# A fused attention and two-expert kernel: another order in the first pairs, decoding spread over the pair, a free bank for the second h, and half of w1 through DRAM

## The chip, the cores and the metric

The kernel runs on one core of a Trainium2 chip. Its engines are TensorE (PE in the profile: matrix products and transposes into PSUM banks), VectorE (DVE), ScalarE (ACT), GpSimd (POOL) and SyncE (SP, which only issues DMAs here). The metric is the device time of one execution, in microseconds (us); the time of a kernel is the median of three runs.

## The reference, cut to what matters

Attention with a memory term, and behind it two experts in a row. All arrays come as 64-bit floats.

```python
# q, k, v (4, 8, 576, 64), M_prev (4, 8, 64, 64), z_prev (4, 8, 64), beta (8)
scores = where(causal, -1e9, scale * q @ k.T)      # causal is the part above the diagonal
a = exp(scores - scores.max(-1)); a /= a.sum(-1) + 1e-9
phi = lambda x: where(x > 0, x, exp(x) - 1) + 1
mem = (phi(q) @ M_prev) / ((phi(q) * z_prev).sum(-1) + 1e-6)
g = 1 / (1 + exp(-beta))
x = heads_to_columns(g * mem + (1 - g) * (a @ v))  # 2304 tokens x 512

h = x @ w_in                                       # w_in 512 x 2048
x = (h * tanh(softplus(h))) @ w_out                # w_out 2048 x 512

out = ((x @ w1) * (x @ w2)) @ w3 @ w_out2          # w1, w2 512 x 1024; w3 1024 x 1024; w_out2 1024 x 512
```

## The kernel before

**Attention.** The 32 heads are worked in 16 pairs `p`, one round of the loop at L568 each; a round computes the scores of pair p and, between them, the transposes and the value products of pair p - 1. The rows of scores come in blocks of 128 queries: `s_blocks` (L402) makes blocks 3, then 2, then 0 and 1 together, `s_last` (L418) the 64 queries that are left of both heads (s4). PE writes the products into a bank pair of psA; DVE takes them with one custom instruction that adds the mask and finds the minimum (`maxed`, L395), ACT makes the exponential and its sum (`expd`, L400), and `normed` (L373) scales each block by the reciprocal of its sum, on DVE or, for four of them, on POOL (L384). `pt_g` (L443) transposes the scaled blocks on PE into psF, and ACT copies them (L452). `pv` (L454) multiplies by v and splits the result into x's high and low half (L473 and L474).

The memory term: `phi_terms` (L332) makes phi(q) with ACT (L340), POOL (L341), DVE (L342) and the product with z on POOL (qz, L345), which is held back behind the last scaling on POOL (`scaled`); `phi_norm` (L350) sums (L354), takes the reciprocal (L356), applies the gate (L357) and multiplies on POOL (phie, L360); `trans_phi` (L365) transposes it. `prep` (L316) transposes q and k of the next pair into psX, ACT copies them (L318), and POOL masks the last queries (qd, L324).

**Weights.** A 64-bit word is made into a 32-bit float by six DVE operations (L110, 111, 114, 117, 120, 121) and one POOL addition (L125); the result is then rounded to a high half (L76) and the rest taken as a low half (L79 or L170), both on POOL, since every product of the experts is made of three products of such halves. One job is a block of 128 rows by 512 columns. The eight jobs of the first quarter of w_in and w_out are done in pairs 4 to 11, one in each, by `drip` (L551): it takes a job's operations from the list `parts` and places some of them behind the DVE instruction in `taken`, the last take of scores. The words lie in two buffers `draw`, the decoded block in one buffer `da` (`decoder(at, 2, 1)`).

**The experts.** The first expert runs in four quarters `g` of 512 hidden columns by six chunks `n` of 384 tokens: `h_steps` (L478) makes h in four parts m, each of twelve products into half of a psA bank pair, and applies the function on ACT and DVE (L498 to 511); `split_y` splits it; `emit_x2` (L660) multiplies by w_out and DVE adds into x2 (L675, L677). Beside it `run(pre, ...)` decodes weights of the second expert into DRAM (`predecode`, L189: w_out2 and the first halves of w1 and w2), and `fold` (L682) multiplies w3 by w_out2 in the last quarter and sends the product through DRAM into `wft`. In the second expert `emit_ab` (L807) makes a and b from x2's halves and the slots w12t of w1 and w2, `emit_out` (L826) the output, five steps later. The second halves of w1 and w2 are decoded straight into the slot by `second_half` (L194), two jobs at each call of `by_two` (L150), between the end of the first expert and the first steps of the second.

**The order.** Each engine works through its instructions in one fixed order. A scheduler sets it from the program, and `tc.issue_after(x)` tells it that what is recorded in the block comes behind x. `in_turn` (L68) does so on PE with its last product, if `ordered[0]` is set, which it is from pair 1 on. PSUM has the tags A (two pairs of banks), X (two banks) and F (two banks).

Of the kernel before, what the change touches and what calls it, by code (L numbers as in the profile page):

```python
# [21 lines left out]
def fused_kernel(ctx: ExitStack, tc, q, k, v, M_prev, z_prev, beta, w_in, w_out, w1, w2, w3, w_out2, out):  # L22
# [8 lines left out]
    NQ = 4  # L31
# [118 lines left out]
    def by_two(jobs):  # L150
        for _ in range(4):
            run(jobs, 2)
            yield
# [33 lines left out]
    w2_dram = dram.tile([2, DM, WN], F32, name="w2_dram")  # L187

    def predecode():  # L189
# [34 lines left out]
    decoder(at, 2, 1)  # L224
# [107 lines left out]
    def phi_terms(p):  # L332
# [58 lines left out]
    scaled = [None]  # L391
    copied = [None]
# [61 lines left out]
    def pv(p):  # L454
# [16 lines left out]
        for o, q0, q1 in ((pm, 0, 512), (pl, 512, S)):  # L471
            x = xl[b // 2][:, :, c, S * (b % 2) + q0:S * (b % 2) + q1]
            nc.scalar.copy(out=x[:, 0], in_=o[:, 0:q1 - q0])  # L473
            sub(x[:, 1], o[:, 0:q1 - q0], x[:, 0])  # L474
# [3 lines left out]
    def h_steps(u):  # L478
# [72 lines left out]
    def drip(n):  # L551

        if not parts and ahead:
            r, done = ahead.pop(0)
            ops, a, flat = decode_ops(r)

            def last():
                ops[6]()
                done(a, flat)

            parts.extend(ops[0:6] + [last])
        with tc.issue_after(taken[0]):
            for op in parts[:n]:
                op()
        del parts[:n]

    pre = predecode()
    for p in range(NPAIR + 1):  # L568

        now, old, new = p < NPAIR, p > 0, p + 1 < NPAIR  # L570
        ordered[0] = 1 <= p
# [9 lines left out]
        decodes = 4 <= p < 12  # L581
# [9 lines left out]
        if old:  # L591
            in_turn(pt_g, p - 1, 1)
            in_turn(pt_g, p - 1, 0)
            if not now:
                in_turn(next, h0)
        if now:
            in_turn(s_blocks, p, (2,))
            if old:
                with tc.issue_after(taken[0]):
                    normed(p - 1, [(4, None)])  # L600
                    phi_norm(p)
        if p == 0:
            gate_values(b_)
# [5 lines left out]
        if new:  # L609
            in_turn(prep, p + 1, "q")  # L610
        if old:
            in_turn(pt_g, p - 1, 3)
        if now:
            in_turn(s_blocks, p, (0, 1))
            if decodes:
                drip(1)
        if new:
            in_turn(prep, p + 1, "k")
        if old:
            in_turn(pt_g, p - 1, 5)  # L620
            in_turn(pt_g, p - 1, 6)
            if not now:
                in_turn(next, h0)
        if p == 1:
            in_turn(trans_phi, 0)
# [5 lines left out]
        if p == 0:  # L631
# [11 lines left out]
        if decodes:  # L643
            drip(7)
# [15 lines left out]
    def emit_x2(u, beside):  # L660
# [4 lines left out]
        for m in range(KD):  # L665
            o = bank("X" if g == NQ - 1 else "XF"[m % 2])[:, 0:CH]
# [65 lines left out]
    def w_slot(s):  # L732
        t = xp.tile([128, 2, 2, KD, 512], F32R, tag=f"xs{s}", name="w12t", padded_shape=[128, 2, 2, KD, S])
        if s == 0:
            for i, wd in enumerate((w1_dram, w2_dram)):
                from_dram(t[:, i], wd)
        w1t[s], w2t[s] = t[:, 0], t[:, 1]
        return t

# [4 lines left out]
    for u in [(g, n) for g in range(NQ) for n in range(NCH)]:  # L744
        g, n = u
        last = g == NQ - 1
        if u not in gt:
# [5 lines left out]
        if last and n == 3:  # L753
            w_slot(0)
        if prev is not None:
            with tc.issue_after(emit_x2(prev, folding if last and n > 0 else pre0)):
                split = split_y(u, y)
        with tc.issue_after(split):
# [4 lines left out]
            if g in (1, 2) and n in (0, 2):  # L763
# [15 lines left out]
    rest = by_two(second_half(w_slot(1)))  # L779
    emit_x2(prev, islice(rest, 1))  # L780
# [64 lines left out]
    for k, (c, m) in enumerate(work):  # L845
# [10 lines left out]
        if k < 3:  # L856
            steps(rest, 1)
# [38 lines left out]
```

## Time and profile before

| | us |
|---|---|
| median of three runs | 1013.98 (1013.22 to 1014.81) |
| the profiled execution, its own time | 1015.02 |
| its span in the trace | 1013.2 |

The busy time of each engine in the span, from the page:

| engine | busy us | share | instructions |
|---|---|---|---|
| PE | 973.4 | 96% | 5584 |
| DVE | 605.5 | 60% | 1380 |
| ACT | 500.8 | 49% | 1016 |
| POOL | 331.8 | 33% | 329 |

The shares are means over stages that differ: attention until about 250 us, the first expert until about 740 us, the second behind it. DVE is busy 60 to 90 per cent in most of the attention and the first expert and 10 to 30 per cent in the second. What sets the time of a stage is read from the waits in it.

### The profile page before, as it was taken

What the parts mean: (1) busy time and instruction counts of PE and PEld (TensorE: products, weight loads), DVE (VectorE), ACT (ScalarE), POOL (GpSimd) and SP (SyncE); (2) the same over time, 40 slices, a digit from 0 to 9 for tenths busy, and PEclk for the clock granted to TensorE, in tenths of its full rate; (3) what the DMA queues carried; (4) which work ended last, traced back from release to release, by engine and by line L of the source; (5) the groups of instructions that cost most, each with busy time, mean ns of one, the idle gap of its engine ahead of it and who ended that gap; (6) DMA issues with size and microseconds to landing.
All of it is one profiled execution on the core that took longest, in us unless ns stands there. A gap on an engine that the chain in (4) does not pass through costs nothing.

```text
span 1013.2 us, 15098 instructions
## 1 busy us (share of the span) xinstructions
PE 973.4 (96%) x5584; PEld 826.9 (82%) x5584; DVE 605.5 (60%) x1380; ACT 500.8 (49%) x1016; POOL 331.8 (33%) x329
## 2 busy tenths in 40 slices
PE   6899889999999999999999999999879999999998
PEld 4565555567999999999999999988658888888897
DVE  4678888873657578967896666666973121121111
ACT  5788788886655555555656544432322221221112
POOL 4456677752252536453545111112540000000000
PEclk8999999999999999999999999999999999999999
DMA  7534443301221233223321672222500100100101
GB/s 155 121 72 95 117 119 86 81 15 63 83 81 45 84 125 123 85 98 111 125 84 63 228 260 73 83 79 79 177 21 0 42 1 1 43 1 5 38 1 63
DMA packets 93626, 81.73 MB, mean 81 GB/s; under 512 B 68720, under 2 KB 72816, under 8 KB 93552
## 3 DMA queue, kind: packets, MB, share of 16 engines
q1 hardware_dynamic: 92224, 80.44, 26.2%
q8 instruction: 44, 0.72, 0.3%
q10 hardware_dynamic: 1328, 0.33, 0.2%
q14 instruction: 30, 0.25, 0.1%
HBM read 65.54 MB, written 15.20 MB: 80 GB/s over the span
## 4 chain that ended last, share of the span: by engine, by line
PE 71%; DVE 12%; POOL 7%; ACT 6%; issue 2%; DMA 2%; POOLq 0%; SPq 0%; DVEq 0%; ACTq 0%
PE psA L63 37%; PE psX L63 17%; PE psF L63 14%; ACT s L400 2%; POOL s L384 2%; DVE s L395 2%; POOL da L125 2%; PE psF L66 1%; DMA draw<-in_moe_w_dram 1%; DVE da L117 1%; DVE da L110 1%; POOL qz L345 1%; ACT pt L452 1%; DVE da L111 1%; DVE da L114 1%
## 5 line engine op out<-in xcount | busy, mean ns | idle before, releaser
L63 PE MATMUL psA<-xt,wqt 128*128 128x384 f32 x1152 | 207.4, 335 | 2.3 <-DVE y L511 2.2
L125 POOL TENSOR_TENSOR da<-da,draw 128x512 f32<-128x512 f32 x72 | 100.8, 1407 | 325.2 <-DVE draw L121 283.0
L63 PEld LDWEIGHTS psA<-xt,wqt 128*128 128x128 f32 x1152 | 200.1, 188 | 3.8 <-DVE y L511 3.1
L63 PE MATMUL psX<-gh,wqt 128*128 128x384 f32 x480 | 122.2, 335 | 1.1 <-DVE x L677 1.1
L822 DVE TENSOR_TENSOR bs<-bs,psA 128x512 f32<-128x512 f32 (+1 forms) x40 | 25.3, 633 | 161.7 <-ACT bs L821 161.7
L63 PE MATMUL psA<-x2h,w12t 128*128 128x512 f32 (+1 forms) x384 | 108.3, 360 | 6.9 <-DVE bs L822 4.6
L821 ACT COPY bs<-psA 128x512 f32<-128x512 f32 (+1 forms) x40 | 21.8, 545 | 163.3 <-PE psA L63 153.4
L400 ACT ACTIVATE s<-s,acc 128x512 f32<-128x512 f32 (+2 forms) x144 | 85.2, 597 | 19.2 <-DVE acc L395 18.3
L63 PE MATMUL psA<-x2s,w12t 128*128 128x512 f32 x384 | 89.6, 389 | 0.0
L63 PEld LDWEIGHTS psX<-gh,wqt 128*128 128x128 f32 x480 | 86.8, 188 | 2.3 <-DVE x L677 1.4
L63 PEld LDWEIGHTS psA<-x2h,w12t 128*128 128x128 f32 x384 | 69.0, 191 | 21.1 <-DVE bs L822 5.0
L498 ACT ACTIVATE y<-psA 128x384 f32<-128x384 f32 x96 | 42.0, 490 | 88.8 <-PE psA L63 88.7
L63 PEld LDWEIGHTS psA<-x2s,w12t 128*128 128x128 f32 x384 | 72.1, 188 | 15.0
L511 DVE TENSOR_TENSOR y<-y,psA 128x384 f32<-128x384 f32 x96 | 48.5, 548 | 54.2 <-ACT y L509 54.2
L63 PE MATMUL psX<-gl,wqt 128*128 128x384 f32 x240 | 80.3, 335 | 0.0
L395 DVE CUSTOM_DVE_ANT_0 s<-psA,mask 128x512 f32<-128x512 f32 (+2 forms) x144 | 63.4, 482 | 25.8 <-PE psA L63 25.5
L66 PEld LDWEIGHTS psF<-ident,s 128*128 128x128 f32 x400 | 44.1, 143 | 41.3 <-ACT pt L452 11.9
L66 PE MATMUL psF<-ident,s 128*128 128x128 f32 x400 | 62.9, 289 | 10.8 <-DVE s L384 6.2
L63 PE MATMUL psF<-gh,wqt 128*128 128x384 f32 x288 | 73.0, 334 | 0.0
L384 POOL TENSOR_SCALAR s<-s,sum,ogp 128x128 f32<-128x128 f32 (+1 forms) x64 | 53.6, 849 | 46.3 <-DVE sum L380 30.5
L63 PE MATMUL psA<-room,w12t 128*128 128x512 f32 (+1 forms) x192 | 68.6, 357 | 0.0
L452 ACT COPY pt<-psF 128x512 f32<-128x512 f32 (+1 forms) x112 | 58.5, 543 | 13.3 <-PE psF L66 13.3
(117 smaller groups left out, 1866.7 us busy)
## 6 DMA issues: line engine op xcount, KB each, us to landing
draw<-in_moe_w_dram SPq DMA_DIRECT2D x32, 512.0 KB, 3.8
draw<-in_moe_w_out_dram SPq DMA_DIRECT2D x24, 512.0 KB, 3.6
draw<-in_moe_w_in_dram SPq DMA_DIRECT2D x16, 512.0 KB, 4.6
out_dram<-ob SPq DMA_DIRECT2D x18, 256.0 KB, 2.0
raw<-in_q_dram SPq DMA_DIRECT2D x32, 128.0 KB, 2.8
raw<-in_v_dram SPq DMA_DIRECT2D x32, 128.0 KB, 2.7
o_dram<-draw SPq DMA_DIRECT2D x8, 512.0 KB, 2.8
w_dram<-draw SPq DMA_DIRECT2D x8, 512.0 KB, 2.9
```

The source lines that it names most:

```text
L63: tail[0] = nc.tensor.matmul(o, lhsT=l, rhs=r, start=start, stop=stop).ins
L66: tail[0] = nc.tensor.transpose(o, src, ident).ins
L110: lambda: V.tensor_scalar(out=ai, in0=hw, scalar1=0x7FFFFFFF, scalar2=None, op0=ALU.bitwise_and),
L125: lambda: nc.gpsimd.tensor_tensor(out=a, in0=a, in1=lw.bitcast(F32), op=ALU.add),
L384: r = (nc.gpsimd if x in ON_POOL else nc.vector).tensor_scalar(out=s, in0=s, scalar1=d["sum"][:, x:x + 1], scalar2=og[:, x:x + 1], op0=ALU ...
L395: taken[0] = nc.vector.tensor_tensor_reduce(out=s, in0=o, in1=m, op0=ALU.add, op1=ALU.min, scale=-scale, scalar=init, accum_out=a,).ins
L400: nc.scalar.activation(out=s, in_=s, func=AF.Exp, scale=-1.0, bias=a, accum_out=r)
L452: copied[0] = nc.scalar.copy(out=t[:, 0:n], in_=o[:, 0:n]).ins
L498: nc.scalar.activation(out=y[m // 2][:, m % 2], in_=hp[m], func=AF.Tanh, scale=0.5)
L511: nc.vector.tensor_tensor(out=y[i][:, j], in0=y[i][:, j], in1=hp[2 * i + j], op=ALU.mult)
L821: nc.scalar.copy(out=bs, in_=pb)
L822: nc.vector.tensor_tensor(out=bs, in0=bs, in1=pa, op=ALU.mult)
```

## The change

- **First pairs.** In pair 0, phi of pair 0 and the transposes of q and k for pair 1 are placed between the scores; qz of pair 0 is not held back behind a scaling; PE's order is fixed from pair 0 on; `trans_phi(0)` moves to the front of pair 1. The block scalings of a pair are placed behind the last take of scores.
- **Decoding in the pairs.** `drip` places the first three operations behind the scores of blocks 0 and 1, the fourth behind the split of x in `pv`, the fifth behind block 3 of the next pair, and the sixth with POOL's three behind block 2 of the next pair. There are two buffers `da`.
- **Second h.** The first part m of h for (g, n) = (0, 1) goes into a psX bank; the other three follow in psA. `emit_x2` of (0, 0) uses the banks X, F, F, X. In the last round of the pair loop one step of the first h moves ahead of `pt_g` 5 and 6.
- **w1's second half.** Its four jobs become part of `predecode`, into a new array `w1b_dram` (written job by job, read back by two DMAs). The number of jobs of `predecode` grows from 16 to 20 and `run(pre, 1)` is called at more chunks. What `second_half` still decodes is w2's four jobs; its slot is taken at the last chunk of the last quarter, and its steps alternate there with those of `fold` (`both`).

The core of the diff; what is left out are the moved calls of the pair loop, which the orders below show.

```diff
     def by_two(jobs):
-        for _ in range(4):
+        for _ in range(2):
...
+        for c in range(KD):
+            yield words(w1, 128 * c, WN), to_dram(w1b_dram[:, 128 * c:128 * c + 128, 0:WN])
...
     def second_half(t):
-        for i, w in ((1, w2), (0, w1)):
-            for c in range(KD):
-                yield words(w, 128 * c, WN), to_split(t[:, i, 0, c], t[:, i, 1, c])
+        for c in range(KD):
+            yield words(w2, 128 * c, WN), to_split(t[:, 1, 0, c], t[:, 1, 1, c])
...
-    decoder(at, 2, 1)
+    decoder(at, 2, 2)
...
-        with tc.issue_after(scaled[0]):
+        with ExitStack() as k_:
+            if p > 0:
+                k_.enter_context(tc.issue_after(scaled[0]))
...
         for m in range(KQ):
-            if m % 2 == 0:
-                two = psA()
-            o = two[:, m % 2, 0:CH]
+            j = m - (u == (0, 1))
+            if j < 0:
+                o = psX()[:, 0:CH]
+            else:
+                if j % 2 == 0:
+                    two = psA()
+                o = two[:, j % 2, 0:CH]
...
         if now:
             in_turn(s_blocks, p, (3,))
-            if decodes:
-                drip(1)
+            drip(1, taken[0])
+            if p == 1:
+                in_turn(trans_phi, 0)
...
+        else:
+            gate_values(b_)
+            phi_terms(0)
+            in_turn(prep, 1, "q")
         if now:
             in_turn(s_blocks, p, (2,))
-            if old:
-                with tc.issue_after(taken[0]):
+            drip(2, taken[0])
+            with tc.issue_after(taken[0]):
+                if old:
                     normed(p - 1, [(4, None)])
-                    phi_norm(p)
+                phi_norm(p)
...
         if now:
             in_turn(s_blocks, p, (0, 1))
-            if decodes:
-                drip(1)
-        if new:
+            if 4 <= p < 12:
+                begin()
+                drip(3, taken[0])
+        if old and new:
             in_turn(prep, p + 1, "k")
...
             in_turn(s_last, p)
-            if decodes:
-                drip(1)
-            normed(p, [(i, e) for e in range(2) for i in range(4)])
-        if p == 0:
             with tc.issue_after(taken[0]):
-                phi_terms(0)
-                phi_norm(0)
+                normed(p, [(i, e) for e in range(2) for i in range(4)])
         if old:
             in_turn(pv, p - 1)
+            drip(1, split_x[0])
...
-            o = bank("X" if g == NQ - 1 else "XF"[m % 2])[:, 0:CH]
+            o = bank("X" if g == NQ - 1 else "XFFX"[m] if u == (0, 0) else "XF"[m % 2])[:, 0:CH]
...
+        else:
+            from_dram(t[:, 0], w1b_dram)
...
+        if last and n == NCH - 1:
+            rest = by_two(second_half(w_slot(1)))
+            beside = both(folding, rest)
...
-            if g in (1, 2) and n in (0, 2):
+            if g in (1, 2) and n == 0 or not last and n in (2, 4):
                 run(pre, 1)
...
-    rest = by_two(second_half(w_slot(1)))
-    emit_x2(prev, islice(rest, 1))
+    emit_x2(prev, rest)
...
-        if k < 3:
-            steps(rest, 1)
```

In the orders that follow the line numbers of after are a few higher: L395 is L400, L360 is L364, L345 is L349, L341 is L343, L324 is L326, L384 is L388.

DVE in pair 4 before, from the takes of block 3 (512 columns) on; draw and da are the job's words and its block, sum and dn belong to the scaling and the memory term:

```order
L395 ISA s_896,acc<-psA,mask 128x512
L395 ISA acc 128x1
L395 ISA s_899,acc<-psA,mask 128x512
L395 ISA acc 128x1
L110 TENSOR_SCALAR da<-draw 128x512
L395 ISA s_921,acc<-psA,mask 128x384
L395 ISA acc 128x1
L395 ISA s_924,acc<-psA,mask 128x384
L395 ISA acc 128x1
L379 TENSOR_SCALAR sum<-sum 128x1
L354 TENSOR_REDUCE dn<-qz 128x10
L380 RECIPROCAL sum<-sum 128x1
```

DVE after, in the same pair, from the takes of blocks 0 and 1 (128 and 256 columns) to that of s4 (s_114):

```order
L400 ISA s_975,acc<-psA,mask 128x128
L400 ISA acc 128x1
L400 ISA s_978,acc<-psA,mask 128x128
L400 ISA acc 128x1
L400 ISA s_981,acc<-psA,mask 128x256
L400 ISA acc 128x1
L400 ISA s_984,acc<-psA,mask 128x256
L400 ISA acc 128x1
L110 TENSOR_SCALAR da<-draw 128x512
L111 TENSOR_SCALAR da<-da 128x512
L114 TENSOR_SCALAR da<-da 128x512
L400 ISA s_114,acc<-psA,mask 128x288
```

Before, L110 stood alone between the blocks of 512 and 384 columns, and L111 and L114 at two later places; after, the three stand in a row between the blocks of 256 columns and s4.

POOL in a decoding pair before, from qz of one pair to the first scaling of the next; wqt is the weight's halves:

```order
L345 TENSOR_TENSOR qz<-phie,zr 128x640
L125 TENSOR_TENSOR da<-da,draw 128x512
L76 TENSOR_SCALAR wqt<-da 128x512
L79 TENSOR_TENSOR wqt<-da,wqt 128x512
L341 TENSOR_SCALAR phit<-raw 128x640
L360 TENSOR_TENSOR phie<-phie,dn 128x640
L324 TENSOR_TENSOR qd<-qt,own 128x128
L384 TENSOR_SCALAR s_1177<-s_1177,sum,ogp 128x128
```

The same after:

```order
L349 TENSOR_TENSOR qz<-phie,zr 128x640
L125 TENSOR_TENSOR da<-da,draw 128x512
L343 TENSOR_SCALAR phit<-raw 128x640
L76 TENSOR_SCALAR wqt<-da 128x512
L326 TENSOR_TENSOR qd<-qt,own 128x128
L364 TENSOR_TENSOR phie<-phie,dn 128x640
L79 TENSOR_TENSOR wqt<-da,wqt 128x512
L388 TENSOR_SCALAR s_1176<-s_1176,sum,ogp 128x128
```

The three operations of the job stood in a row before; after, phit, qd and the phie product stand between them, and the subtraction L79 comes behind the phie product.

PE at the start before: the transposes of q and k (raw) into psX, the scores of pair 0 (kt, qt), and the first of pair 1:

```order
L66 MATMUL psX<-ident,raw 128x128 x12
L63 MATMUL psA<-kt,qt 128x512 x2
L63 MATMUL psA<-kt,qt 128x384 x2
L66 MATMUL psX<-ident,raw 128x128 x5
L63 MATMUL psA<-kt,qt 128x128 x2
L63 MATMUL psA<-kt,qt 128x256 x2
L63 MATMUL psA<-kt,qd 128x288 x2
L66 MATMUL psX<-ident,raw 128x128 x3
L63 MATMUL psA<-kt,qt 128x512 x2
L66 MATMUL psF<-ident,s_242 128x128
```

The same after:

```order
L66 MATMUL psX<-ident,raw 128x128 x10
L63 MATMUL psA<-kt,qt 128x512 x2
L66 MATMUL psX<-ident,raw 128x128 x5
L63 MATMUL psA<-kt,qt 128x384 x2
L66 MATMUL psX<-ident,raw 128x128 x5
L63 MATMUL psA<-kt,qt 128x128 x2
L63 MATMUL psA<-kt,qt 128x256 x2
L63 MATMUL psA<-kt,qd 128x288 x2
L63 MATMUL psA<-kt,qt 128x512 x2
L66 MATMUL psX<-ident,phie 128x128 x2
L66 MATMUL psF<-ident,phie 128x128 x3
L66 MATMUL psF<-ident,s_266 128x128
```

The transposes for pair 1 now stand in two fives between the score products of pair 0, and those of phi for pair 0 come ahead of the first scaled block. At the end of the first expert, in the order of PE, the last products of `fold` stood behind 48 products with w12t before and stand behind 95 after; in both 48 or 49 such products follow them before the first one with wft.

## Rows read from the trace of the kernel before

**Rows 1.** Waits of PE from 0 to 290 us: total us, times, longest.

```profile
PE psF L66 <- DVE s L384: 6.2, 8, 0.8
...
PE psA L63 <- DVE y L511: 2.2, 1, 2.2
```

**Rows 2.** Timeline of PE, the first product of three pairs: start, us, instruction.

```profile
39.94 1.13 PE L63 MATMUL psA<-kt,qt 64*128 64x512 f32 x4
...
67.24 1.13 PE L63 MATMUL psA<-kt,qt 64*128 64x512 f32 x4
...
198.99 1.13 PE L63 MATMUL psA<-kt,qt 64*128 64x512 f32 x4
```

**Rows 3.** Windows: us, busy PE, PEld, DVE, ACT, POOL, PEclk, DMA, GB/s.

```profile
53.59:67.24 13.65, 13.21 (x103) 8.27 (x102) 10.05 (x38) 11.67 (x35) 6.99 (x9) 1.00 0.34 78
95.68:110.60 14.92, 13.49 (x103) 8.22 (x103) 12.72 (x43) 11.88 (x35) 10.77 (x12) 1.00 0.44 107
```

**Rows 4.** The same of a stretch in the first expert.

```profile
405.00:557.00 152.00, 151.90 (x875) 151.16 (x874) 122.37 (x220) 86.19 (x118) 70.98 (x64) 1.00 0.28 95
```

**Rows 5.** Waits of PE from 290 us to the end.

```profile
PE psA L63 <- DVE bs L822: 4.6, 3, 3.0
PE psA L63 <- POOL w12t L76: 2.1, 3, 1.5
...
PE psX L63 <- DVE wft L79: 0.9, 1, 0.9
```

**Rows 6.** Timeline of PE in pair 1.

```profile
20.05 1.54 PE L66 MATMUL psF<-ident,s 128*128 128x128 f32 x6 [0.80 <-POOL s L384]
21.52 1.65 PE L63 MATMUL psA<-kt,qt 64*128 64x384 f32 x4
```

**Rows 7.** Timeline of DVE in pairs 1 and 2.

```profile
22.83 0.82 DVE L354 TENSOR_REDUCE dn<-qz 128x10 f32<-128x640 f32 x1 [2.08 <-POOL qz L345]
...
25.24 0.55 DVE L395 CUSTOM_DVE_ANT_0 s<-psA,mask 128x384 f32<-128x384 f32 x1
...
42.98 0.56 DVE L395 CUSTOM_DVE_ANT_0 s<-psA,mask 128x384 f32<-128x384 f32 x1 [0.56 <-PE psA L63]
```

**Rows 8.** Windows at the start, columns as in rows 3.

```profile
15.30:19.50 4.20, 1.79 (x7) 0.58 (x6) 3.10 (x12) 2.39 (x9) 1.28 (x2) 1.00 0.74 169
19.50:26.30 6.80, 6.09 (x23) 4.28 (x23) 4.59 (x15) 2.94 (x7) 5.75 (x6) 0.50 0.74 167
```

**Rows 9.** Timeline of DVE in a decoding pair.

```profile
102.82 0.94 DVE L110 TENSOR_SCALAR da<-draw 128x512 int32<-128x512 int32 x1 [1.75 <-POOL wqt L79]
...
105.67 0.67 DVE L111 TENSOR_SCALAR da<-da 128x512 f32<-128x512 f32 x1
```

**Rows 10.** Timeline of POOL in the same pair.

```profile
99.41 1.31 POOL L125 TENSOR_TENSOR da<-da,draw 128x512 f32<-128x512 f32 x1
...
101.52 1.27 POOL L79 TENSOR_TENSOR wqt<-da,wqt 128x512 fp32r<-128x512 f32 x1
...
104.80 1.26 POOL L360 TENSOR_TENSOR phie<-phie,dn 128x640 f32<-128x640 f32 x1 [1.31 <-DVE dn L357]
```

**Rows 11.** Timeline of DVE, the same operation with POOL idle.

```profile
655.84 0.42 DVE L110 TENSOR_SCALAR da<-draw 128x512 int32<-128x512 int32 x1
```

**Rows 12.** Timeline of DVE in the last stage of decoding.

```profile
714.71 0.84 DVE L110 TENSOR_SCALAR da<-draw 128x512 int32<-128x512 int32 x1
715.59 1.39 DVE L111 TENSOR_SCALAR da<-da 128x512 f32<-128x512 f32 x1
```

**Rows 13.** Timeline of POOL in the same stretch.

```profile
714.65 0.62 POOL L76 TENSOR_SCALAR w12t<-da 128x512 fp32r<-128x512 f32 x1
715.36 1.34 POOL L79 TENSOR_TENSOR w12t<-da,w12t 128x512 fp32r<-128x512 f32 x1
```

**Rows 14.** Timeline of ACT at the start of the second expert.

```profile
752.24 2.18 ACT L804 CAST x2s<-x 128x512 fp32r<-128x512 f32 x4 [16.92 <-POOL w12t L79]
```

**Rows 15.** Timeline of PE behind it.

```profile
756.04 0.50 PE L63 MATMUL psA<-x2h,w12t 128*128 128x512 f32 x1 [3.05 <-DVE bs L822]
```

More of the change, by code (lines that the diff above doesn't have):

```diff
@@ L187, in fused_kernel @@
     w2_dram = dram.tile([2, DM, WN], F32, name="w2_dram")
+    w1b_dram = dram.tile([2, DM, WN], F32, name="w1b_dram")
     def predecode():
@@ L391, in fused_kernel @@
     scaled = [None]
+    split_x = [None]
     copied = [None]
@@ L473, in pv @@
             nc.scalar.copy(out=x[:, 0], in_=o[:, 0:q1 - q0])
-            sub(x[:, 1], o[:, 0:q1 - q0], x[:, 0])
+            split_x[0] = sub(x[:, 1], o[:, 0:q1 - q0], x[:, 0]).ins
     gt = {}
@@ L549, in fetch_next, with begin, last, drip @@
             ahead.append((fetch(src), done))
[L551 to L561, printed above, removed]
-        with tc.issue_after(taken[0]):
+    def begin():
+        r, done = ahead.pop(0)
+        ops, a, flat = decode_ops(r)
+        def last():
+            ops[6]()
+            done(a, flat)
+        parts.extend(ops[0:6] + [last])
+    def drip(n, behind):
+        with tc.issue_after(behind):
             for op in parts[:n]:
@@ L570, in fused_kernel @@
         now, old, new = p < NPAIR, p > 0, p + 1 < NPAIR
-        ordered[0] = 1 <= p
+        ordered[0] = True
         if old:
@@ L595, in fused_kernel @@
                 in_turn(next, h0)
+        else:
+            gate_values(b_)
+            phi_terms(0)
+            in_turn(prep, 1, "q")
         if now:
             in_turn(s_blocks, p, (2,))
-            if old:
-                with tc.issue_after(taken[0]):
+            drip(2, taken[0])
+            with tc.issue_after(taken[0]):
+                if old:
                     normed(p - 1, [(4, None)])
-                    phi_norm(p)
-        if p == 0:
-            gate_values(b_)
+                phi_norm(p)
         if old:
@@ L608, in fused_kernel @@
                 in_turn(next, h0)
-        if new:
-            in_turn(prep, p + 1, "q")
-        if old:
+            if new:
+                in_turn(prep, p + 1, "q")
             in_turn(pt_g, p - 1, 3)
+            if not now:
+                in_turn(next, h0)
+        else:
+            in_turn(prep, 1, "k")
         if now:
             in_turn(s_blocks, p, (0, 1))
-            if decodes:
-                drip(1)
-        if new:
+            if 4 <= p < 12:
+                begin()
+                drip(3, taken[0])
+        if old and new:
             in_turn(prep, p + 1, "k")
@@ L621, in fused_kernel @@
             in_turn(pt_g, p - 1, 6)
[L622 to L625, printed above, removed]
         if now:
             in_turn(s_last, p)
-            if decodes:
-                drip(1)
-            normed(p, [(i, e) for e in range(2) for i in range(4)])
-        if p == 0:
             with tc.issue_after(taken[0]):
-                phi_terms(0)
-                phi_norm(0)
+                normed(p, [(i, e) for e in range(2) for i in range(4)])
         if old:
             in_turn(pv, p - 1)
+            drip(1, split_x[0])
         if not now:
@@ L736, in w_slot, with both @@
                 from_dram(t[:, i], wd)
+        else:
+            from_dram(t[:, 0], w1b_dram)
         w1t[s], w2t[s] = t[:, 0], t[:, 1]
         return t
+    def both(a, b):
+        while True:
+            next(a, None)
+            yield
+            next(b, None)
+            next(a, None)
+            yield
     folding = fold()
@@ L746, in fused_kernel @@
         last = g == NQ - 1
+        beside = folding
         if u not in gt:
@@ L754, in fused_kernel @@
             w_slot(0)
+        if last and n == NCH - 1:
+            rest = by_two(second_half(w_slot(1)))
+            beside = both(folding, rest)
         if prev is not None:
-            with tc.issue_after(emit_x2(prev, folding if last and n > 0 else pre0)):
+            with tc.issue_after(emit_x2(prev, beside if last and n > 0 else pre0)):
                 split = split_y(u, y)
```

3 lines of the change are left out of this document (removed).

## The prediction

> **What bounds the kernel now.** First the waits of PE (TensorE) up to 290 us: it loses 6.2 us in eight waits of transposes (psF) for VectorE's scaled scores, and 2.2 us once where the second h waits for VectorE to empty a psA bank [rows 1]. Then where PE starts each pair: pair 2 at 39.94 us, pair 4 at 67.24, pair 13 at 198.99 [rows 2]. The windows of one plain and one decoding pair show what a pair is limited by [rows 3]: a plain pair takes 13.65 us with PE busy 13.21, so PE sets it; a decoding pair takes 14.92 with PE busy only 13.49 and DVE (VectorE) at 12.72. Nine pairs from 67.24 to 198.99 take 131.75 us; nine plain ones would take 122.85. So decoding costs 8.90 us on the path. In the expert layers PE is the whole story: from 405 to 557 us it is busy 151.90 of 152.00 us [rows 4]. After 290 us it waits again only late: 4.6 us for DVE's bs, 2.1 and 0.9 us for w12t and wft [rows 5].
>
> **Start, pairs 0 and 1.** The edit moves phi of pair 0 and the q and k of pair 1 ahead, so the chain qz, sum, reciprocal and scaling no longer stands in pair 1. In the trace PE has finished pair 1's 384-column scores at 21.52 + 1.65 = 23.17 us, but DVE, which waited 2.08 us for qz and then ran the chain from 22.83, takes them at 25.24 [rows 6, 7]. A regular pair has them taken 42.98 - 39.94 = 3.04 us after its start [rows 2, 7], and the next pair starts 13.65 - 3.04 = 10.61 us after that. In the new order the chain (the 2.41 us between the rows at 22.83 and 25.24, with one instruction more among them) stands in pair 0 ahead of DVE's last scores there, and I charge 1.0 us of it, an estimate, since DVE had some room. Then the six transposes that began at 20.05 begin near 21.05, take 0.8 us at full clock (1.54 at half), the 384-column product about as much, and DVE takes it at 22.9. Pair 2 would start at 22.9 + 10.6 = 33.5: 6.4 us earlier. Against it stands the clock: after a stretch in which PE was busy 1.79 of 4.20 us, the granted clock was 0.50 (1.2 GHz) for 6.80 us [rows 8]. The new order has the same kind of holes there, around 16 and 20 us (a hole is only shifted by the same 1.0 us). 6.80 us at half speed is 3.4 us of work, so if all of it counts, the gain is 3.0. I take -5.0, range -6.4 to 0 (0 if the strict order of PE, which now begins in pair 0, gives the rest away).
>
> **Decoding in the pairs.** Six DVE operations and three POOL ones decode one 128x512 block per pair. Before, one of six stands ahead of the scaling of s4; it waits 1.75 us for POOL's last subtraction (L79, begun 101.52), since there is one da buffer, then lasts 0.94 instead of 0.42 us [rows 9 to 11]. With two buffers the 1.75 us goes. If that were all, DVE's own work would be 12.72 - 0.52 (the 0.94) - 0.25 (L111, 0.67 against the same 0.42) = 11.95 us, well under 13.65, and PE would set the pair again.
>
> But the new place puts the three operations L110, L111, L114 behind each other, right where POOL now has qd, the phie product and the L79 subtraction in a row. What such neighbours do to each other is in the trace: L110 at 714.71 took 0.84 us and L111 at 715.59 1.39 [rows 12], where alone one takes 0.42 [rows 11]. POOL's L76 ran from 714.65 to 715.27 and its L79 from 715.36 to 716.70 [rows 13]: each DVE operation ended 0.28 us after the POOL one did, and POOL got in between two DVE operations that follow each other. L111 at 105.67 beside the phie product of 104.80 (ended 106.06) lasted 0.67 [rows 9, 10]: the same. So in the new pair I let DVE and POOL alternate: L110 waits for qd (0.4), L111 for the phie product (1.26), L114 for L79 (1.27) [rows 10]. Further, L121 releases POOL's L125 (1.31) at once, and the scaling of s4, some 1.0 us of DVE work later, meets it: 0.4. L117 and L120 meet POOL's scaling and qz: 0 to 1.0, I take 0.4. Sum: 11.95 + 0.4 + 1.26 + 1.27 + 0.4 + 0.4 = 15.7 us, bounds 14.7 (L110 gets in before qd, the last term nothing) and 16.3. That is DVE's own round, and it exceeds PE's 13.65, so the pair takes it. The chain is tied: POOL's row begins when L121 ends, so a later DVE only takes POOL along. Pair 4 has no such round yet and pair 12 no first three operations, so seven rounds count: 7 x (15.7 - 13.65) = 14.4 against today's 8.9: +5.5 us. With 13.65 it is -8.9, with 16.3 +9.7.
>
> The Trainium skill ("SBUF — State Buffer", section "Who interferes with whom") says that the port pair which VectorE and GpSimd share is an exclusive lock: a VectorE instruction in a two-port mode, or one with two SBUF inputs against a GpSimd instruction that reads SBUF, blocks fully until the other is done. The rows at 714 to 717 us agree. It says that whichever starts first holds the pair, and not who is next; if VectorE kept it over three instructions in a row, only the first would wait, which is the rival below, with its time from rows.
>
> **Handoff to the experts.** The second h begins in a free psX bank: twelve products stand before the first that needs the emptied psA bank. The 2.2 us [rows 1] is the whole wait, and twelve products (151.90 / 875 = 0.174 us each, in a row as dense as that of [rows 4]) cover 2.1 of it; the last bank of the product behind (psX again) is free before PE comes to it by my reading, by 0.5 us or so. -2.0, bounds -2.2 and 0.
>
> **w1's second half through DRAM.** Four jobs of eight move from the last stage into the first three quarters of the experts: per job six DVE and three POOL operations, one fetch, and new are one write of 512 KB per job and two reads of 1 MB. There PE waited for nothing [rows 4], and no step gets more than the three jobs that some have today, so I cost them at 0; if a step's cover fails, PE waits for a weight, some 1 us each. In the last stage half of the decoding goes. What waited for it: w12t 2.1, and the split x2s, which started at 752.24 only when POOL had finished the last job, and made PE wait 3.05 us at 756.04 [rows 5, 14, 15]. With the rest of DVE's waits and wft, 4.6 + 2.1 + 0.9 = 7.6 us are at stake. What is late next: the folded weights. By the order of PE the last folding product moves from behind 48 to behind 95 of the w12t products, and eleven us of products lie between it and the first use of wft, about what that took before. I take -6.5, bounds -8 and -2.
>
> **Sum.** -5.0 + 5.5 - 2.0 - 6.5 = -8.0. The profiled execution took 1015.02 us (span 1013.2 and 1.8 around it), 1.04 above the median 1013.98 of the runs and 0.21 above the slowest of them; I set the sum against it, 1007.0, and carry the difference to the median: 1006.0.
>
> **Rivals.**
> - *The spreading fits.* DVE keeps its turn over the three operations, or POOL is not ready; the pair takes 13.65 to 14.1, at 13.9 seven rounds cost 1.8 instead of 8.9: -7.1. Total -5.0 - 7.1 - 2.0 - 6.5 = -20.6: 993.4. For it: 11.95 us of work and a gap in plain pairs; against it: [rows 12, 13].
> - *Alternation, and one of the early or late gains is missing* (half clock and strict order eat the start, or folded weights arrive late): -8.0 + 5.0 to 6.0: about 1011.5. For it: the fold's moved end and the half clock [rows 8]; against: half the jobs are gone.
> - *DVE rounds of 18 us.* If POOL's scaling, too, is pushed behind each VectorE operation, the scaled s3 comes late to PE and the round stretches beyond 17.2 us; from there on decoding costs 7 x 3.55 - 8.9 = 16 us more, and outweighs the 13.5 us of the other edits by 0.2%. At 17.7 the total is 7 x 4.05 - 8.9 - 13.5 = +6: 1020. For it: at 714 to 717 two operations in a row lost 1.4 us; against: POOL has only six operations to put between.
>
> **Chances.** Alternation with all gains 0.55 (its own range 1001 to 1011), fitting 0.25, a missing gain 0.13, rounds of 18 us 0.07. The range 991 to 1012.5 leaves out the rounds of 18 us, the lowest part of the fitting case and the top of the third. About 0.2% (2 us) is what can be told from no change. Faster: 0.53 of the first, 0.25, and 0.05 of the third, 0.83; within: 0.10; slower: 0.07.
>
> **What would show it.** Right: in the changed profile L111 and L114 last 1.2 to 1.7 us in decoding pairs and end 0.3 us after a POOL product; pairs 5 to 11 are 15 to 16 us apart; pair 2 starts at 33 to 37 us; no wait of psA for y at 240 to 260; x2s splits before 730. Wrong: decoding pairs 13.7 us apart with 0.42 us operations (the first rival), or pair 2 at 40, or PE waiting over 3 us for wft.

## The result and the profile after

The changed kernel takes 1000.71 us (median of four runs, 999.95 to 1001.74), the kernel before beside it 1013.6; the ratio is 0.9871, with a 95% interval of 0.9854 to 0.9889. The forecast was 1006.0 in a range of 991 to 1012.5, and faster. The span of the profiled execution fell from 1013.2 to 998.9 us, by 14.3; the medians differ by 12.9.

Where the 14.3 us of the profiled executions went is read from the starts of the same PE instruction in both traces. The timeline of PE after, at pairs 2, 4 and 13 (rows of before: [rows 2]), at the third h, (0, 2), and at the h of (3, 1), the second chunk of the last quarter:

```profile
33.40 1.13 PE L63 MATMUL psA<-kt,qt 64*128 64x512 f32 x4
...
60.69 1.13 PE L63 MATMUL psA<-kt,qt 64*128 64x512 f32 x4
...
197.73 1.13 PE L63 MATMUL psA<-kt,qt 64*128 64x512 f32 x4
...
269.91 8.48 PE L63 MATMUL psA<-xt,wqt 128*128 128x384 f32 x48
...
556.16 8.59 PE L63 MATMUL psA<-xt,wqt 128*128 128x384 f32 x48
```

The last two in the kernel before:

```profile
273.60 8.48 PE L63 MATMUL psA<-xt,wqt 128*128 128x384 f32 x48
...
557.34 8.48 PE L63 MATMUL psA<-xt,wqt 128*128 128x384 f32 x48
```

The lead is 6.55 us at pair 4 (67.24 - 60.69), 1.26 at pair 13, 3.69 at the third h, 1.18 at the h of (3, 1) and 14.3 at the end. The differences are the terms of the forecast's sum:

| stage | forecast (bounds) | measured |
|---|---|---|
| start, to pair 4 | -5.0 (-6.4 to 0) | -6.55 |
| decoding, pairs 4 to 12 | +5.5 (-8.9 to +9.7) | +5.29 |
| handoff, to the third h | -2.0 (-2.2 to 0) | -2.43 |
| first expert, to the h of (3, 1) | 0 | +2.51 |
| from there to the end | -6.5 (-8 to -2) | -13.12 |
| sum | -8.0 | -14.30 |

The windows of a plain and of a decoding pair after (columns as in [rows 3], to which they answer):

```profile
60.69:74.34 13.65, 13.21 (x103) 8.28 (x103) 11.49 (x41) 11.66 (x35) 7.17 (x9) 1.00 0.34 78
119.10:134.77 15.67, 13.49 (x104) 8.25 (x103) 15.48 (x42) 11.60 (x35) 10.81 (x11) 1.00 0.41 102
```

The decoding pair is now DVE's: busy 15.48 of 15.67 us, with one instruction fewer than in [rows 3], where 12.72 were busy. The extra time lies in longer instructions. DVE in that pair:

```profile
123.26 1.31 DVE L120 TENSOR_SCALAR draw<-da 128x512 int32<-128x512 int32 x1
...
126.10 0.80 DVE L358 TENSOR_REDUCE dn<-qz 128x10 f32<-128x640 f32 x1
...
126.94 0.57 DVE L359 TENSOR_SCALAR dn<-dn 128x10 f32<-128x10 f32 x1
127.42 1.07 DVE L388 TENSOR_SCALAR s<-s,sum,ogp 128x576 f32<-128x576 f32 x1
...
129.66 1.22 DVE L110 TENSOR_SCALAR da<-draw 128x512 int32<-128x512 int32 x1
130.91 1.38 DVE L111 TENSOR_SCALAR da<-da 128x512 f32<-128x512 f32 x1
132.32 0.43 DVE L114 TENSOR_SCALAR da<-da 128x512 int32<-128x512 int32 x1
```

And POOL beside it:

```profile
122.73 1.54 POOL L349 TENSOR_TENSOR qz<-phie,zr 128x640 f32<-128x640 f32 x1
126.19 1.28 POOL L125 TENSOR_TENSOR da<-da,draw 128x512 f32<-128x512 f32 x1 [1.93 <-DVE sum L383]
127.45 0.72 POOL L343 TENSOR_SCALAR phit<-raw 128x640 f32<-128x640 f32 x1
...
129.34 1.25 POOL L364 TENSOR_TENSOR phie<-phie,dn 128x640 f32<-128x640 f32 x1
130.56 1.45 POOL L79 TENSOR_TENSOR wqt<-da,wqt 128x512 fp32r<-128x512 f32 x1
```

Each lengthened DVE operation ends shortly after a POOL one: L120 at 124.57 (qz at 124.27), L359 at 127.51 (L125 at 127.47), the scaling of s4 at 128.49 (phit at 128.17), L110 at 130.88 (the phie product at 130.59), L111 at 132.29 (L79 at 132.01). L114 follows with POOL idle and takes 0.43. Between L110 and L111, which stand next to each other, POOL got its turn.

PE's waits after, up to 290 us and then from there on (total, times, longest; they answer to [rows 1] and [rows 5]):

```profile
PE psF L66 <- DVE xt L79: 7.6, 7, 1.1
...
PE psF L66 <- DVE s L388: 3.8, 8, 0.6
```

```profile
PE psA L63 <- DVE y L520: 1.0, 2, 0.6
```

In the attention PE now waits about 1.1 us in each of seven pairs for DVE's split of x, which stands behind the late scalings; the 2.2 us for y at the handoff are gone, and so are all the waits of the last stage (the two that are left for y lie in the first expert). ACT's split of x2, which answers to [rows 14], now begins 21 us earlier:

```profile
730.93 2.19 ACT L824 CAST x2s<-x 128x512 fp32r<-128x512 f32 x4
```

At the start, the windows of after over the stretch of [rows 8]:

```profile
15.30:17.18 1.88, 0.69 (x3) 0.22 (x2) 1.81 (x12) 1.29 (x7) 1.78 (x2) 1.00 0.89 203
17.18:19.50 2.32, 1.82 (x9) 0.82 (x9) 2.16 (x9) 2.32 (x9) 0.34 (x2) 1.00 0.66 153
19.50:26.30 6.80, 5.87 (x39) 3.75 (x39) 5.69 (x20) 5.34 (x14) 5.12 (x7) 1.00 0.73 165
```

From 15.30 to 19.50 PE is busy 0.69 + 1.82 = 2.51 us and not 1.79, the granted clock stays at 1.00 (2.4 GHz), and 39 products fit where 23 stood. DVE takes pair 1's 384-column scores here:

```profile
22.85 0.56 DVE L400 CUSTOM_DVE_ANT_0 s<-psA,mask 128x384 f32<-128x384 f32 x1 [1.08 <-PE psA L63]
```

It waits for PE there; in [rows 7] PE's scores waited for it. The transposes ahead of these scores begin 1.04 us later than in [rows 6]:

```profile
21.09 0.87 PE L66 MATMUL psF<-ident,s 128*128 128x128 f32 x6 [0.79 <-POOL s L388]
```

### The profile page after: what moved, and what is told of

It reads as the page before. It is cut to its first block, busy times and chain, and to the rows that moved or that the text cites. A ratio compares the mean times of both kernels' runs of the same rounds, so it can differ in the third digit from the quotient of the medians.

```text
span 998.9 us, 15097 instructions
## 1 busy us (share of the span) xinstructions
PE 966.7 (97%) x5584; PEld 823.6 (82%) x5584; DVE 639.1 (64%) x1380; ACT 498.4 (50%) x1016; POOL 331.1 (33%) x329
## 4 chain that ended last, share of the span: by engine, by line
PE 63%; DVE 25%; ACT 6%; issue 2%; DMA 2%; SPq 1%; POOL 1%; ACTq 0%; DVEq 0%; POOLq 0%
PE psA L63 34%; PE psX L63 15%; PE psF L63 12%; DVE da L117 3%; DVE s L400 3%; DVE draw L120 3%; DVE da L111 3%; DVE da L114 2%; DVE s L388 2%; DVE da L110 2%; ACT s L405 2%; DVE y L520 2%; DVE draw L121 2%; PE psF L66 1%; DVE gl L79 1%
## 5 line engine op out<-in xcount | busy, mean ns | idle before, releaser
L125 POOL TENSOR_TENSOR da<-da,draw 128x512 f32<-128x512 f32 x72 | 99.0, 1381 | 311.9 <-DVE draw L121 231.8
L63 PEld LDWEIGHTS psA<-xt,wqt 128*128 128x128 f32 x1140 | 197.7, 188 | 4.4 <-DVE y L520 3.6
L63 PE MATMUL psA<-x2h,w12t 128*128 128x512 f32 (+1 forms) x384 | 105.4, 354 | 0.0
L400 DVE CUSTOM_DVE_ANT_0 s<-psA,mask 128x512 f32<-128x512 f32 (+2 forms) x144 | 63.4, 477 | 24.4 <-PE psA L63 24.0
L388 POOL TENSOR_SCALAR s<-s,sum,ogp 128x128 f32<-128x128 f32 (+1 forms) x64 | 53.1, 840 | 45.9 <-DVE sum L384 43.9
```

The lines of the kernel that those rows point to most:

```text
L63: tail[0] = nc.tensor.matmul(o, lhsT=l, rhs=r, start=start, stop=stop).ins
L125: lambda: nc.gpsimd.tensor_tensor(out=a, in0=a, in1=lw.bitcast(F32), op=ALU.add),
L388: r = (nc.gpsimd if x in ON_POOL else nc.vector).tensor_scalar(out=s, in0=s, scalar1=d["sum"][:, x:x + 1], scalar2=og[:, x:x + 1], op0=ALU ...
L400: taken[0] = nc.vector.tensor_tensor_reduce(out=s, in0=o, in1=m, op0=ALU.add, op1=ALU.min, scale=-scale, scalar=init, accum_out=a,).ins
```

## The experiments

Each edit is against the changed kernel ("after"), each ratio against the kernel before, run beside it. After itself, run once more beside runs 9 and 10, took 1001.56 us, a ratio of 0.9862 (0.9838 to 0.9885).

> The changed kernel unaltered, beside the two others on one chip: 1000 to 1002.

**1. The decoding undone, old places and one buffer.**

```diff
-    decoder(at, 2, 2)
+    decoder(at, 2, 1)
...
-            drip(1, taken[0])
+            if 4 <= p < 12:
+                begin()
+                drip(1, taken[0])
...
-            drip(2, taken[0])
...
-                begin()
-                drip(3, taken[0])
+                drip(1, taken[0])
...
             in_turn(s_last, p)
+            if 4 <= p < 12:
+                drip(1, taken[0])
...
-            drip(1, split_x[0])
...
                 phi_terms(p + 1)
+        if 4 <= p < 12:
+            drip(7, taken[0])
```

> The changed kernel with the decoding part alone undone: one da buffer, and the six operations at their places of before. Theory (the spread places cost 2.0 us in each of seven pairs because DVE and POOL take turns, where before L110's wait for the one da buffer cost 1.2 us in each): pairs 14.9 us apart again, pair 13 some 5.3 us earlier than in the changed kernel, time 995.4. Rival (the longer pairs come from the new start or the fixed order from pair 0 on): decoding pairs stay at 15.7, time 1000.7.

Measured: 997.07 us, ratio 0.9811 (0.9786 to 0.9836). Pairs are 14.9 us apart and pair 13 starts at 192.50, 5.23 us earlier than in after: the theory. The time gained is only 3.6 to 4.5 us by the medians (3.6 by the spans of the traces), since behind 551 us this kernel was 1.4 us slower: the scheduler set the folding otherwise, and PE waits once 0.9 us for its decoded words.

**2. Old places, two buffers.** The same without the first hunk.

> As the run before, but with the two da buffers. Theory: the 1.75 us wait of L110 for POOL's subtraction goes, DVE's own work is about 12 us, PE sets the decoding pairs again at 13.65 to 13.9 us, time 986.5 to 989. Rival (DVE and POOL still take turns somewhere in the pair, so the wait only changes its place): pairs of 14.5 us or more, time 993 to 995.

Measured: 991.15 us, ratio 0.9753 (0.9733 to 0.9774). That lies between the theory and the rival. L110's wait is gone, pairs take 14.05 to 14.10 us, and the window says why:

```profile
116.21:130.26 14.05, 13.26 (x103) 8.24 (x102) 13.98 (x44) 11.97 (x35) 11.22 (x12) 1.00 0.44 114
```

DVE is busy throughout. The theory's 12 us of its own work was too low: L110, L111 and L361 last 1.02, 1.14 and 1.00 us here, each ending shortly after a POOL product. So the second buffer alone is worth 5.9 us against the run before it, and the spread places cost 9.6 to 10.4 us more by the medians than the old ones with the same two buffers.

**3. The three operations behind s4.**

```diff
-            if 4 <= p < 12:
-                begin()
-                drip(3, taken[0])
...
             in_turn(s_last, p)
+            if 4 <= p < 12:
+                begin()
+                drip(3, taken[0])
```

> The changed kernel with L110, L111 and L114 recorded behind the take of s4 and not ahead of it, where POOL has ended its subtraction and waits for the sums. All else as in the changed kernel, the same number of DVE operations in a pair. Theory (neighbours on POOL lengthen them): L110 and L111 last 0.42 to 0.6 us and not 1.22 and 1.38, decoding pairs 13.9 to 14.3 us, time 988 to 992. Rival (the sheer DVE work of a pair sets it, or the scaled scores now come late to PE): pairs stay at 15.5 or more, time 1000 or more.

Measured: 992.57 us, ratio 0.9768 (0.9747 to 0.9788); pairs of 14.23 us. DVE in such a pair:

```profile
126.97 0.77 DVE L110 TENSOR_SCALAR da<-draw 128x512 int32<-128x512 int32 x1
...
128.47 0.41 DVE L111 TENSOR_SCALAR da<-da 128x512 f32<-128x512 f32 x1
...
128.91 0.42 DVE L114 TENSOR_SCALAR da<-da 128x512 int32<-128x512 int32 x1
```

And the POOL operation that is still beside the first of them:

```profile
126.18 1.27 POOL L79 TENSOR_TENSOR wqt<-da,wqt 128x512 fp32r<-128x512 f32 x1
```

The same three operations take 1.60 and not 3.03 us, with POOL's neighbours gone from two of them (L110 again ends 0.29 us after L79). DVE's busy time in the whole pair falls from 15.48 to 13.52 us, though no operation was removed:

```profile
116.25:130.47 14.22, 13.27 (x103) 8.26 (x102) 13.52 (x43) 11.86 (x35) 10.58 (x12) 1.00 0.47 112
```

This is the run that shows the cause of the longer pairs: not the number of DVE operations, but who stands beside them.

**4. The second h in psA.**

```diff
-            j = m - (u == (0, 1))
+            j = m
...
-            o = bank("X" if g == NQ - 1 else "XFFX"[m] if u == (0, 0) else "XF"[m % 2])[:, 0:CH]
+            o = bank("X" if g == NQ - 1 else "XF"[m % 2])[:, 0:CH]
```

> The changed kernel with the second h in psA alone and the banks X, F, X, F of before. Theory: PE waits 2.2 to 2.4 us again for DVE to empty psA at the second h, time 1003.1. Rival (the step of the first h that moved ahead of the last transposes brought the 2.4 us, not the free bank): time 1000.7.

Measured: 1004.55 us, ratio 0.9882 (0.9859 to 0.9906). PE's wait is back:

```profile
254.57 3.76 PE L63 MATMUL psA<-xt,wqt 128*128 128x384 f32 x20 [2.30 <-DVE y L520]
```

From pair 13 to the third h it needs 74.17 us (after: 72.18, before: 74.61). So the free bank brings 2.0 of the 2.43 us; the other 0.4 is, by difference, the moved step. The median rose by more than the theory's 2.4 us, by 3.8; why is open.

**5. w1's second half straight into the slot.** The hunks on `by_two`, `predecode`, `second_half`, `from_dram`, `rest` and the third jobs undone:

```diff
-            if g in (1, 2) and n == 0 or not last and n in (2, 4):
+            if g in (1, 2) and n in (0, 2):
...
-    emit_x2(prev, rest)
+    rest = by_two(second_half(w_slot(1)))
+    emit_x2(prev, islice(rest, 1))
```

> The changed kernel with w1's second half decoded straight into the slot at the end, as before (eight jobs behind the first expert, sixteen in predecode, the third job of a chunk at fewer chunks). Theory (the late gain is 13.5 us: 8.9 us of PE's waits and some 4.6 us that PE works more slowly behind each wait; the moved jobs cost 2.9 us in the first expert): first expert 2.9 us shorter, the stage behind it 13.5 longer, time 1011.3. Rival (only the waits count, 8.9, and the rest of the late gain has another cause in the change): time 1006.7.

Measured: 1011.48 us, ratio 0.9963 (0.995 to 0.9975). Against after that is 10.8 us by the medians and 9.3 by the ratios, nearer to the theory (10.6) than to the rival (6.0). The trace is of an execution of 1009.42 us. In it the stretch from the h of (3, 1) to the end takes 453.73 us (after 442.74, before 455.86): 11.0 us are w1's jobs, between the rival's 8.9 and the theory's 13.5. The waits of PE there add up to 8.4 us, before's to 8.9 (the 7.6 named in the prediction, 1.1 for x2 and 0.2 for w12t from L79). The other 2.6 us are lost at the edges of the waits. PE in after, where it never waits, and behind one of the waits in this run:

```profile
751.47 5.60 PE L63 MATMUL psA<-x2s,w12t 128*128 128x512 f32 x24
756.91 0.84 PE L63 MATMUL psX<-wft,room 128*128 128x512 f32 x3
```

```profile
744.58 0.84 PE L63 MATMUL psF<-wft,room 128*128 128x512 f32 x3
746.91 0.50 PE L63 MATMUL psA<-x2h,w12t 128*128 128x512 f32 x1 [1.49 <-POOL w12t L76]
747.25 0.39 PE L63 MATMUL psA<-room,w12t 128*128 128x512 f32 x1
747.48 0.40 PE L63 MATMUL psA<-x2h,w12t 128*128 128x512 f32 x1
```

In after 24 products start (756.91 - 751.47) / 24 = 0.227 us apart. Behind the wait they do so again from the second one on (747.25 to 747.48), but the first has 0.34 us to its successor, 0.11 more. Ahead of the wait three products are listed with 0.84 us, 0.16 more than 3 x 0.227, since the end of the last one, as the profile models it, is not covered by a successor. So a wait costs some 0.27 us beyond its listed length, and the nine waits 2.4 of the 2.6 us. Before needs 2.1 us more than this run: 0.5 of waits, and the rest where its granted clock fell:

```profile
756.00:760.00 4.00, 3.96 (x11) 3.14 (x12) 1.93 (x3) 1.82 (x3) 0.00 (x0) 0.60 0.01 4
```

A granted clock of 0.60 over 4.00 us, part of it at 1.2 GHz, takes away 1.6 us of work. It fell there behind the wait of 3.05 us for bs [rows 15]; behind the same wait in this run it did not fall, and why is open.

In the first expert the run shows the other side. Its window of the h of (1, 0) to that of (1, 1), and after's of the same chunk and of the one two further on:

```profile
336.63:353.27 16.64, 16.64 (x97) 16.64 (x97) 10.82 (x22) 9.50 (x13) 6.59 (x6) 1.00 0.28 96
```

```profile
336.55:353.44 16.89, 16.81 (x98) 16.49 (x97) 16.58 (x25) 8.67 (x12) 7.99 (x7) 1.00 0.41 144
...
370.19:387.64 17.45, 16.80 (x98) 16.49 (x97) 16.68 (x25) 8.67 (x12) 8.01 (x7) 1.00 0.52 175
```

PE needs 16.64 us for a chunk, and DVE with three jobs 16.6: no slack is left. What PE waits for stands in the rows of its weight loads (PEld), which the list of PE's waits above leaves out. From 290 to 560 us, before and after in turn:

```profile
PEld psA L63 <- DVE y L511: 0.7, 2, 0.4
```

```profile
PEld psA L63 <- DVE y L520: 3.6, 7, 1.0
```

Each of these waits is at the start of an h, for which DVE has not yet emptied psA. Of after's eight chunks with three jobs the first takes 16.64 us and the others 16.87 to 17.45 (in the two longest DVE also waits 0.5 and 0.2 us for words from DRAM); of before's four, two take 16.64 and two about 16.86. A three-job chunk that loses nothing follows one with only two jobs; the others follow a chunk into which the job of the one before still reaches. Over the 17 chunks from the third h to the h of (3, 1), the time beyond 16.64 us each is 0.86 us before, 3.37 after and 0.92 in run 5.

**6. The old start.**

```diff
-        ordered[0] = True
+        ordered[0] = 1 <= p
...
-            gate_values(b_)
-            phi_terms(0)
-            in_turn(prep, 1, "q")
...
+        if p == 0:
+            with tc.issue_after(taken[0]):
+                phi_terms(0)
+                phi_norm(0)
```

> The changed kernel with the start of before: phi of pair 0 behind its scores, q and k of pair 1 at the end of pair 0, PE's order fixed from pair 1 on. Theory (the chain through qz in pair 1 and the half clock behind it cost 6.5 us): pair 2 starts at 39.9 and not 33.4, time 1007.2. Rival (part of the 6.5 us is given back further on, in the first decoding pair): time 1004 or less.

Measured: 1007.49 us, ratio 0.992 (0.9893 to 0.9947); pair 2 starts at 39.62. The half clock is back:

```profile
19.50:26.30 6.80, 6.09 (x23) 4.28 (x23) 4.52 (x16) 3.23 (x9) 5.76 (x7) 0.52 0.79 165
```

Nothing is given back later: the lead of after over this run is 6.2 us at pair 4 (66.92 - 60.69) and 6.8 at the end.

**7 and 8. L111 also behind s4; the third job in halves.** Run 7 is run 2 with L111 moved from behind blocks 0 and 1; run 8 adds a split of the third jobs, three operations in their chunk and the rest ahead of the next chunk's two jobs.

```diff
-            if 4 <= p < 12:
-                drip(1, taken[0])
...
             in_turn(s_last, p)
             if 4 <= p < 12:
-                drip(1, taken[0])
+                drip(2, taken[0])
```

```diff
-                run(pre, 1)
+                steps(third, 1)
```

> As the run with the old places and two da buffers, but L111 also behind the take of s4, where POOL waits, so that of the six operations only L110 still meets a POOL product. Theory: DVE's work in a pair falls from 13.98 by 0.7 to 13.3 us, below PE's 13.65, pairs 13.65 to 13.8 us, time 988.2 to 989. Rival (the operation makes the sums and the scaled scores later, and PE waits for them instead): pairs 14.1 us or more, time 991 to 992.

> As the run before, and where a chunk of the first expert decodes three jobs, the third job's last three DVE operations and its POOL ones move into the next chunk, which has two jobs. Theory (the 2.9 us lost in the first expert are chunks in which DVE's work, 16.6 us with three jobs, is as long as PE's 16.64): every chunk takes 16.64 to 16.7 us, 2 to 2.9 us less than the run before. Rival (the loss is DVE's wait for POOL and for da, or the DMAs): no gain, or slower by the longer hold of da.

Both forecasts missed: 994.16 us, ratio 0.9795 (0.9773 to 0.9816), and 995.7 us, 0.9807 (0.9787 to 0.9827). Run 7's pairs take 14.41 us, as its rival had it, with DVE busy 13.74 in one of them: L111 shrank to 0.42, but the scaling of s4 now meets POOL's L79 and lasts 1.68 us (0.57 in run 2), the order changed too (the sixth operation now stands behind the split of x), and from 90 to 190 us PE waits 5.2 us in seven waits for the copies of transposed scores; which of the moved instructions makes these late is open. In run 8 the three-job chunks fell to 16.64 to 16.67, except two in which DVE waits up to 1.0 us for a block of words from DRAM and which still take 17.6. It gains 1.0 us by the h of (3, 1) and loses more behind it, where another order of the folding makes PE wait 1.9 and 1.1 us.

**9, 10 and 12. One job over one and a half pairs.** Twelve pairs from 2 to 13, four DVE operations in each.

```diff
+            for _ in range(n):
+                if not parts:
+                    begin()
+                if parts:
+                    parts.pop(0)()
+                if len(parts) == 1:
+                    parts.pop(0)()
```

Run 12 against run 10:

```diff
-                    parts.pop(0)()
+                    lasts.append(parts.pop(0))
...
+            with tc.issue_after(scaled[0]):
+                for op in lasts:
+                    op()
```

> The changed kernel with two da buffers and the eight jobs spread over the twelve pairs 2 to 13: four DVE operations in each pair (one behind block 3, one behind s4, two at the pair's end) and POOL's three directly behind the sixth. Theory (a pair is prolonged only when DVE's work, with what POOL's products add, passes PE's 13.65 us; with eight jobs in eight pairs and the old places it was 13.98): with four operations DVE has some 12.3 to 13.4 us in a pair, all pairs take 13.65 to 13.8, 2 to 3 us less than the run with old places and two buffers: 988 to 989. Rival (the scaled scores come late in more pairs, as in the run with L111 behind s4): twelve pairs 0.3 to 0.7 us longer, time 992 or more.

> As the run before, but no operation behind block 3 and two behind s4, so that none meets qz or the memory term's products on POOL, and all four stand ahead of or in the scaling. Theory: fewer operations are lengthened, but the sums of the scores come 0.4 to 0.9 us later, so PE waits for scaled scores: 990 to 992, between. Rival (only the amount of DVE's work counts): as the run before or less.

> As the run with no operation behind block 3, but POOL's three operations of a job are placed behind its scaling and the product with z, where that run had them ahead of the scaling in four pairs, which took 14.30 us. Theory (in those four pairs the scaled scores came late because POOL added the words first): all pairs 13.65 to 13.8 us, 2.0 to 2.6 us less, time 988 to 988.6, the fastest version. Rival (a POOL product then stands beside L388 or the memory term on DVE, and the loss only changes its place): 14.1 us or more in those pairs, time 990 or more.

Run 9 took 991.85 us, ratio 0.9766 (0.9739 to 0.9793): four of twelve pairs take 14.59 (PE waits 0.5 us in each for DVE's split of x), the rest 13.65. Run 10 took 990.62 us, 0.9754 (0.9731 to 0.9777), with four pairs of 14.30. POOL at the start of one of those in run 10:

```profile
100.65 1.47 POOL L125 TENSOR_TENSOR da<-da,draw 128x512 f32<-128x512 f32 x1 [4.16 <-DVE draw L121]
102.11 2.96 POOL L388 TENSOR_SCALAR s<-s,sum,ogp 128x128 f32<-128x128 f32 x4
```

POOL adds the words first, and the scaled scores come 1.46 us later. PE waits for them, from 60 to 205 us:

```profile
PE psF L66 <- POOL s L388: 1.7, 4, 0.4
```

In run 12, where that wait is gone, the addition stands behind the scaling:

```profile
100.35 2.94 POOL L388 TENSOR_SCALAR s<-s,sum,ogp 128x128 f32<-128x128 f32 x4 [4.37 <-DVE sum L384]
103.26 1.54 POOL L349 TENSOR_TENSOR qz<-phie,zr 128x640 f32<-128x640 f32 x1
104.77 1.30 POOL L125 TENSOR_TENSOR da<-da,draw 128x512 f32<-128x512 f32 x1
```

Every pair then takes 13.64 to 13.78 us: nine pairs from pair 4 on take 123.20 us, where nine plain ones take 122.85, so decoding costs next to nothing on the path. Run 12 took 988.3 us, ratio 0.9732 (0.9708 to 0.9756), the lowest median of all; the intervals of runs 2, 9 and 10 overlap with its own.

## Why the prediction was right, and where its sizes were off

The direction and the range held; the middle, 1006.0, is 5.3 us too slow, and 1000.71 lies just outside the 1001 to 1011 that the prediction gave to the case that came true. Of the five stages only the decoding lies within its stated bounds. Of the signs, pair 2 (33.40) and the missing wait for y came as named; the long operations are L110 and L111, not L111 and L114, the long rounds are those of pairs 6 to 12, not 5 to 11, and the split of x2 starts at 730.93, not before 730.

- **Start (-5.0; measured -6.55, just past its bound): right in place and chain.** Without the reserve for the clock the working gave 21.05 us for the transposes, 22.9 for DVE's take and 33.5 for pair 2; the trace has 21.09, 22.85 and 33.40. The reserve of 1.5 us was needless: the holes were shorter, and the clock stayed at 1.00.
- **Decoding (+5.5; measured +5.29): right in mechanism, and its near hit is luck.** The pair was forecast at 15.7 and takes 15.67 (15.44 to 15.82), in seven rounds. But the losses stand elsewhere than in the sum. L110 loses 0.80 beside the phie product, where 0.4 beside qd was charged; L111 loses 0.96 beside L79, where 1.26 beside the phie product was charged; L114 loses nothing, where 1.27 was charged, since L79 had taken its turn beside L111. In its place L120 loses 0.9 beside qz and L117 0.2, of which 0.4 was charged for both, and L359 loses 0.4 beside L125 (0.57 us, in run 2 0.17), which was not in the sum. The scaling of s4 (0.50, forecast 0.4) is near. Charged were 3.7 us in all, and lost are 3.8. The lower bound of the pair, 14.7, is a slip: without the two terms of 0.4 the sum is 14.9. Run 3 shows the cause by taking it away. The Trainium skill ("SBUF — State Buffer", section "Who interferes with whom") says also that a reduction never contends with GpSimd on this chip; the trace agrees: L358 takes 0.80 us beside L125, and its like in [rows 7] 0.82 with POOL idle. What was missed is that the old places with two buffers leave the pair at 14.05 to 14.10: removing the wait for `da` was a gain by itself, and the new places lost it again.
- **Handoff (-2.0; measured -2.43, past its bound of -2.2): right,** 2.0 by the bank (run 4).
- **w1's second half, in the first expert (0; measured +2.51): this step failed.** The argument that "no step gets more than the three jobs that some have today" took those steps to be free. They are not: with three jobs DVE's 16.6 us fill the chunk's 16.64, DVE empties psA late, and PE's weight loads wait 3.6 us in seven chunks. The kernel before paid 0.86 us too, around two of its four such chunks, in a stretch that [rows 4] show as busy 151.90 of 152.00 us: there the loss stands as busy time (16.80 us for the chunk from 406.80 instead of 16.64). Run 5 takes w1's jobs away and has 0.92 of the 3.37 us left.
- **The last stage (-6.5; measured -13.12): mis-sized by the factor two, past its bound of -8.** The sum counted 7.6 us of waits and took 6.5 of them. All waits went, 8.9 us with 1.1 for x2 and 0.2 for w12t that were left out, and nothing new came late: the folded weights arrived in time. The other 4.2 us had no term: 2.6 are the edges of the nine waits (run 5, at full clock), and 1.6 the lower granted clock in before.

The errors of the last two steps, one of +2.5 and one of -6.6, partly cancel and add to 4.1 us of gain, the needless reserve to 1.55: that is the whole distance between -8.0 and -14.3 with the 0.4 of the handoff and 0.2 of the decoding. Of the rivals, the one in which the spreading fits names a time (993.4) that other places for the operations pass (runs 2, 3, 9, 10 and 12).

## What to carry to other kernels

Before spreading work over an engine's gaps, look at what its neighbour on the other engine does there: moving three operations, none removed, took a pair from 15.67 to 14.23 us. A wait of PE costs more than its listed length, here some 0.27 us more, so a stage with nine waits is worth more than the table of waits says. PE can also wait in the rows of its weight loads while its products are shown as busy. And a stage in which PE is always busy may already be paying for a second engine that is full: compare the time of one round with and without the extra work, not the busy share.

## What was not expected of the hardware

- Around a wait PE loses some 0.27 us beyond the listed idle time, at full clock: the first product behind it has 0.34 us to the next and not 0.227, and the last one ahead of it ends 0.16 us uncovered.
- Waits of 0.4 to 1.0 us for VectorE to empty a bank showed on PE's weight loads, seven of them, and only two of them also on its products.
- A tiny DVE operation pays beside POOL too: L359 on 128x10 elements took 0.57 us beside POOL's L125, 0.17 without.
- Of two DVE operations that follow each other, POOL gets the turn in between (L110 and L111 lose 0.80 and 0.96 us); where POOL has nothing ready, the third takes 0.43.
